# Part of a streamed weight chunk made resident, paid for with one output-tail buffer and a gathered tail

## The chip, the cores and the metric

The kernel runs on one core of one Trainium2 chip. The metric is the device time of one execution in microseconds (us). Every kernel is timed several times. PE is the matmul engine and PEld its weight loads, DVE, ACT and POOL are the vector, scalar and general engines, SP and the DMA queues move data.

## The reference, cut to what matters

The program has two independent parts. Part A, a long convolution by FFT, takes the first 490 us and is not touched. Part B is a recurrence over 64 segments of 32 new tokens, each with 8 memory tokens in front. Each segment needs the memory that the segment before it has produced:

```python
mem = mem0
for s in range(n_seg):                              # 64 segments, strictly one after the other
    h = jnp.concatenate([mem, x[:, 32*s:32*s+32]], axis=1)
    q, k, v = (jnp.einsum('btd,dhe->bhte', h, W) for W in (Wq, Wk, Wv))   # 1024 -> 32 heads x 128
    p = _softmax(where(mask, q @ k^T * scale, -1e9))
    o = jnp.einsum('bhte,hed->btd', p @ v, Wo)      # 32 heads x 128 -> 1024
    mem = o[:, :M, :]                               # rows of the memory tokens
    outs.append(o[:, M:, :])
```

(The two lines with `for W in` and `k^T` are shortened; the meaning is the reference's.) The kernel is compared with the reference by relative error.

## The kernel before

All weights of part B are 64 chunks of 128x2048 bf16, 512 KB each. 43 are resident in SBUF, and the other 21 are listed in `STREAM`; two of these are parked after their first load (`KEPT`), so each segment streams 19 chunks through a ring of six slots. A slot is refilled as soon as PE has used its chunk:

```python
STREAM = (0, 1, 3, 7, 11, 15, 21, 23, 25, 29, 33, 36, 40, 43, 46, 49, 51, 53, 59, 60, 62)
TURN = (6, 4)
INLINE = {1: 0, 3: 1, 5: 0, 11: 1, 12: 0, 14: 1}     # streamed output chunk -> parity of the segment
RING = 6

def fetch():                                        # next streamed chunk into the next free slot
    if loads:
        s, ch = loads.pop(0)
        live[s, ch] = k, t = slot()
        (...).dma_start(t[:], stream_src(ch))

def done(ch):                                       # PE has used ch: its slot is free, fetch again
    if ch in streamed:
        free.append(live.pop((now[0], ch))[0])
        ...
        fetch()
```

The last 8 new tokens of every segment don't depend on the memory, so their projections are made in advance. A segment in the loop handles the other 32 rows (24 new tokens and the memory). It runs the projections K, Q, K, Q, V, V, eight chunks each (two halves `g` of each, on four column tiles of PE), the attention, and an output projection over 16 chunks into `yacc`. The end of a segment is called the **turn** here: `Y` is cast from `yacc`, transposed, written into the next segment's input, and only then can the next first K projection begin.

The output rows of those last 8 tokens take a separate path, the **tail**. Its input is kept in `OTB`, and it is worked off for two segments together (a block of an even and an odd segment), so that one matmul covers 16 rows. There are 32 **heads** of it; one head is four small matmuls and four weight loads:

```python
def head(self, h, w):                               # class Tail
    for dq in range(4):
        nc.tensor.matmul(self.acc[32*dq:32*dq+W, ...], lhsT=self.OTB[:, c, 4*g+i, :], rhs=r,
                         ..., tile_position=(0, 32*dq))
```

20 heads use resident chunks and can run at any time. 12 use streamed ones and must run **inline**, in an output projection while the chunk is there. Before the change a block's tail is spread over the block that follows: at the odd turn 6 resident heads before the transposes of `Y` and 4 after them, 6 inline heads in the next even segment, 6 + 4 resident heads at the even turn, 6 inline heads in the next odd segment. That needs two `OTB` buffers.

```python
# out_proj, after the eight matmuls of a chunk
if tail is not None and 2*hp in tail.left and (ch in streamed or last):
    if last or INLINE[hp] == j:                     # j is 0 in even, 1 in odd segments
        tail.head(2*hp, w); tail.head(2*hp+1, w)
...
nc.scalar.copy(Y[:], yacc[:, 0:256])                # the turn
if j == NB - 1 and not last:
    tail = Tail(OTB, b)                             # its constructor clears the accumulator (DVE)
if tail is not None and not last:
    tail.run(TURN[0])                               # 6 resident heads
if not last:
    fill_mem(pend[s + 1][0], Y)                     # transposes of Y on PE, copy into the next input
...
if tail is not None and not last:
    tail.run(TURN[1])                               # 4 resident heads
```

The scores accumulator and the tail's accumulator share one PSUM tile, `SB`. It is seeded with the mask on DVE (`seed_scores`), before the change at the end of each softmax.

## Time and profile before

| | before |
|---|---|
| time, median of 4 runs | 2195.29 us (2187.41 to 2197.44) |
| span of the profiled run, granted clock | 2190.4 us, 0.971 |
| one segment of the loop | 26.8 us |
| bytes moved by DMA | 804.66 MB |

The first fence is from the page of before: the span, the busy time of PE (with its share and its instruction count), and the DMA rows of the 40 time slices, where a digit is the busy share in tenths.

```profile
span 2190.4 us, 81498 instructions
...
PE 1734.6 (79%) x35636; PEld 927.5 (42%) x35636; DVE 872.0 (40%) x2686; ACT 648.4 (30%) x1139; POOL 436.8 (20%) x1131
...
DMA  9998879889999999999999999999999999999996
GB/s 324 340 341 295 267 274 391 277 293 383 388 379 392 393 356 385 392 391 395 392 387 385 393 391 391 394 395 374 396 393 374 388 383 384 389 394 392 394 389 263
DMA packets 262702, 804.66 MB, mean 367 GB/s; under 512 B 52332, under 2 KB 52364, under 8 KB 262343
```

The reader sees DMA at nine tenths all through the loop and PE busy for 79% of the span. The windows view of the loop (1000 to 2000 us) gives the rate more finely; after the busy times come the granted clock, the DMA share and GB/s:

```profile
1000.00:2000.00 1000.00, 809.80 (x19875) 462.04 (x19867) 362.25 (x1303) 256.27 (x485) 178.99 (x567) 0.99 1.01 389
```

The waits view of before, from 600 to 2100 us (28 blocks), lists what ended an engine's idle time, with the total, the number of times and the longest one. L884 is a projection's matmul, L970 the output projection's, L830 a tail head's, L809 the seeding, L821 the clearing of the tail's accumulator. "issue" means that the profile shows nothing that the engine waited for.

```profile
engine line waited for: us in total, times, longest us
...
PEld L884 <- issue: 214.6, 385, 2.2
...
PEld L970 <- issue: 132.9, 176, 1.9
PE acc L884 <- DMA wring<-WS: 102.6, 233, 1.9
...
PE yacc L970 <- DMA wring<-WS: 47.5, 91, 1.1
...
PE SB L830 <- DVE SB L809: 27.8, 28, 1.2
...
PE yacc L970 <- issue: 23.6, 26, 1.6
...
PE SB L830 <- DVE SB L821: 18.3, 26, 0.7
```

PE waits for streamed chunks.

The last fence is the timeline of before around one odd turn. Columns are the start, the duration, the engine, line and operation, and in brackets the idle time before it with its releaser.

```profile
1696.11 0.37 ACT L1026 CAST Y<-yacc 128x256 bf16<-128x256 f32 x1 [4.26 <-PE yacc L970]
...
1696.77 0.40 PE L830 MATMUL SB<-Wmore,OTB 128*16 128x256 bf16 x8 [0.71 <-DVE SB L821]
...
1697.54 0.29 PE L791 MATMUL tps<-ident,Y 128*128 128x128 bf16 x2
...
1697.75 0.61 PE L830 MATMUL SB<-Wlate,OTB 128*16 128x256 bf16 x16
...
1698.19 0.60 PE L884 MATMUL acc<-wring,rec 128*32 128x512 bf16 x8
```

Four heads follow the transposes of `Y` with no wait, and fill the time in which DVE copies the transposes into the next input. The next projection starts 0.65 us after the transposes. Ahead of the transposes six heads wait for the clearing of the tail's accumulator (0.71 us).

### The profile page before, as it was taken

Reading aid. Unit: us, or ns where it says so; the run is one execution under the profiler, and the core shown is the slowest. Engines: PE = TensorE matmul, PEld = TensorE weight load, DVE = VectorE, ACT = ScalarE, POOL = GpSimd, SP = SyncE. Lnnn points to the kernel's source line nnn. Section 1 sums busy time; section 2 is a strip of 40 time slices with the busy share of each in tenths; the row PEclk is TensorE's granted clock in tenths of the full one; section 3 lists DMA queues with packets and bytes.
Section 4 is the critical chain, followed back from the end, with each engine's and each line's share of the span. In section 5 each row is a group of like instructions: output and inputs, shape, how many; then the busy total and the mean of one; then the engine's idle time right before and its main releaser. Section 6 shows DMA issues by size and latency. Waiting matters only on the chain. (4 is left out here: it accounts for less than half of the span.)

```text
span 2190.4 us, 81498 instructions
## 1 busy us (share of the span) xinstructions
PE 1734.6 (79%) x35636; PEld 927.5 (42%) x35636; DVE 872.0 (40%) x2686; ACT 648.4 (30%) x1139; POOL 436.8 (20%) x1131
## 2 busy tenths in 40 slices
PE   4688888678878878888887887888878888888886
PEld 2232233234444444444444444444444444444444
DVE  9927752023333333333333333333333333333332
ACT  8935521122222222222222222222222222222221
POOL 4013422311111111111111111111111211111111
PEclk9899999889999999999999999999999999999999
DMA  9998879889999999999999999999999999999996
GB/s 324 340 341 295 267 274 391 277 293 383 388 379 392 393 356 385 392 391 395 392 387 385 393 391 391 394 395 374 396 393 374 388 383 384 389 394 392 394 389 263
DMA packets 262702, 804.66 MB, mean 367 GB/s; under 512 B 52332, under 2 KB 52364, under 8 KB 262343
## 3 DMA queue, kind: packets, MB, share of 16 engines
q1 hardware_dynamic: 230008, 725.84, 86.9%
q0 software_dynamic: 27120, 63.11, 8.4%
q10 hardware_dynamic: 5216, 10.49, 1.3%
q8 instruction: 279, 4.57, 0.8%
q14 instruction: 79, 0.65, 0.1%
HBM read 739.92 MB, written 62.39 MB: 366 GB/s over the span
## 5 line engine op out<-in xcount | busy, mean ns | idle before, releaser
L884 PEld LDWEIGHTS <-rec 128*32 128x32 bf16 x12351 | 324.2, 96 | 477.8 <-issue 259.1
L884 PE MATMUL acc<-wring,rec 128*32 128x512 bf16 (+1 forms) x3777 | 375.9, 386 | 141.6 <-DMA wring<-WS 126.4
L893 ACT CAST qkv_sb<-acc 128x512 bf16<-128x512 f32 x384 | 224.8, 585 | 660.8 <-PE acc L884 660.8
L970 PEld LDWEIGHTS <-OT 128*32 128x32 bf16 x8192 | 216.3, 96 | 178.2 <-issue 151.3
L970 PE MATMUL yacc<-wring,OT 128*32 128x256 bf16 x3072 | 153.9, 275 | 98.0 <-DMA wring<-WS 56.4
L884 PE MATMUL acc<-Wmid,rec 128*32 128x512 bf16 x3072 | 225.8, 383 | 0.0
L884 PE MATMUL acc<-Wres,rec 128*32 128x512 bf16 x2816 | 221.2, 380 | 0.0
L830 PEld LDWEIGHTS <-OTB 128*16 128x16 bf16 x4096 | 105.1, 90 | 105.5 <-issue 95.1
L956 ACT CAST OT<-OTp 128x512 bf16<-128x512 f32 x128 | 74.9, 585 | 242.9 <-PE OTp L948 242.9
L986 DVE COPY KT<-tps 128x512 bf16<-128x512 bf16 x64 | 27.2, 424 | 298.6 <-PE tps L899 298.6
L785 POOL DMA_DIRECT2D rec<-REC x64 | 37.5, 585 | 526.6 <-issue 277.2
L957 DVE CAST OTB<-OTp 128x128 bf16<-128x128 f32 x128 | 37.3, 291 | 262.1 <-ACT OT L956 262.1
L736 DVE TENSOR_SCALAR wring<-OTp 128x384 int32<-128x384 int32 x126 | 112.2, 890 | 58.4 <-PE acc L884 52.4
L884 PE MATMUL acc<-pw,rec 128*32 128x512 bf16 x1536 | 130.4, 382 | 0.0
L860 POOL COPY KT<-rec 128x128 bf16<-128x128 bf16 x128 | 38.6, 302 | 427.8 <-PE SB L908 421.9
L845 POOL DMA_DIRECT2D out_dram<-YB x128 | 73.0, 577 | 234.2 <-DVE YB L843 224.0
L914 DVE TENSOR_REDUCE mx<-SB 128x5 f32<-128x200 f32 x128 | 47.1, 368 | 181.4 <-PE SB L908 181.4
L830 PE MATMUL SB<-wring,OTB 128*16 128x256 bf16 x1488 | 78.2, 273 | 39.1 <-DVE SB L809 31.0
L899 PE MATMUL tps<-ident,qkv_sb 128*128 128x128 bf16 x1024 | 101.0, 221 | 8.0 <-ACT qkv_sb L893 0.2
L899 PEld LDWEIGHTS <-qkv_sb 128*128 128x128 bf16 x1024 | 62.6, 97 | 105.0 <-ACT qkv_sb L893 67.5
L970 PE MATMUL yacc<-Wlate,OT 128*32 128x256 bf16 x2048 | 93.4, 273 | 2.9 <-issue 2.7
L1026 ACT CAST Y<-yacc 128x256 bf16<-128x256 f32 x64 | 23.8, 372 | 242.8 <-PE yacc L970 238.9
(229 smaller groups left out, 2690.1 us busy)
## 6 DMA issues: line engine op xcount, KB each, us to landing
wring<-WS SPq DMA_DIRECT2D x1216, 512.0 KB, 7.4
rec<-REC POOLq DMA_DIRECT2D x64, 192.0 KB, 6.1
SK<-s_sb SPq DMA_DIRECT2D x16, 512.0 KB, 4.9
SU<-s_sb SPq DMA_DIRECT2D x16, 512.0 KB, 5.0
Kg<-SK SPq DMA_DIRECT2D x32, 256.0 KB, 4.5
Ug<-SU SPq DMA_DIRECT2D x32, 256.0 KB, 5.6
REC<-stage POOLq DMA_DIRECT2D x16, 512.0 KB, 9.7
zt<-SZ SPq DMA_DIRECT2D x16, 512.0 KB, 8.7
```

The source lines that it names most:

```text
L736: nc.vector.tensor_scalar(out=dst, in0=src, scalar1=0, scalar2=None, op0=ALU.bitwise_or)
L785: nc.gpsimd.dma_start(rec[:], REC[:, s, :])
L830: nc.tensor.matmul(self.acc[32 * dq:32 * dq + W, x - o:y - o], lhsT=self.OTB[:, c, 4 * g + i, :], rhs=r, start=first and not self.seeded, ...
L845: nc.gpsimd.dma_start(bass.AP(outb.tensor, outb.offset + (SEG * NB * self.b + NX) * 2048 + 256 * dq, [[2048 * SEG, NB], [2048, 8], [1, 256 ...
L860: nc.gpsimd.tensor_copy(KT[:, :, :, 32:40], KBs[:, 128 * g:128 * g + 128].rearrange("p (c i t) -> p i c t", c=4, i=4))
L884: nc.tensor.matmul(self.acc[32 * c:32 * c + 32, x - 512 * c:y - 512 * c], lhsT=hT[:, kc, :], rhs=r, start=(kc == 0 and x == 512 * c), stop ...
L893: nc.scalar.copy(sb[:], self.acc[:])
L899: nc.tensor.transpose(tp[:, i * 128:(i + 1) * 128], sb[:, i * 128:(i + 1) * 128], ident[:])
L914: nc.vector.tensor_reduce(out=mx[:], in_=S, op=ALU.max, axis=AX.X)
L956: nc.scalar.copy(OT[:], o_view[:, :, :, 0:32])
L957: nc.vector.tensor_copy(OTB[:, :, 4 * g:4 * g + 4, 8 * j:8 * j + 8], o_view[:, :, :, 32:40])
L970: nc.tensor.matmul(yacc[32 * dq:32 * dq + 32, x - o:y - o], lhsT=OT[:, c, i, :], rhs=r, start=(h == 0 and x == o), stop=(h == 31), tile_po ...
```

## The change

The intent is to stream fewer bytes. The change makes room in SBUF for 768 of the 2048 columns of one streamed chunk (the third, K projection, `order[3]`). It does so by keeping one `OTB` in place of two, by letting the padded softmax tile share the buffers of QT and KT, and by a pool with one buffer. With one `OTB` a tail must be done before the next even segment writes it. So all 12 inline heads run in the odd segment's own output projection, 4 + 6 resident heads at the odd turn, and the last ten between chunk pairs of the next first K projection. `seed_scores` for the next segment moves from the second softmax to behind `fill_mem`, so that the inline heads don't wait for it.

The core of the diff (the buffer sharing of the softmax tile, the store buffer of its own and the end of the last block are cut):

```diff
-TURN = (6, 4)
-INLINE = {1: 0, 3: 1, 5: 0, 11: 1, 12: 0, 14: 1}
+TURN = (4, 6)
+HALF, HELD = 3, 768
...
+    half = order[HALF]
+    WH = ring.tile([128, HELD], BF, name="WH")
+    nc.gpsimd.dma_start(WH[:], dram_chunk(half)[:, 0:HELD])
...
-            (...).dma_start(t[:], stream_src(ch))
+            c = slice(HELD if ch == half else 0, 2048)
+            eng.dma_start(t[:, c], stream_src(ch)[:, c])
...
+        if ch == half:
+            return [(0, HELD, WH[:]), (HELD, 2048, t[:, HELD:2048])]
...
-                    if tail is not None and 2 * hp in tail.left and (ch in streamed or last):
-                        if last or INLINE[hp] == j:
-                            tail.head(2 * hp, w)
-                            tail.head(2 * hp + 1, w)
+                    if j == NB - 1 and ch in streamed:
+                        tail.head(2 * hp, w)
+                        tail.head(2 * hp + 1, w)
...
-            k0 = Proj(0, 0).run().evac()
+            k0 = Proj(0, 0)
+            for n in (3, 3, 32, 0):
+                k0.run(2)
+                more_tail(n)                        # tail.run(n) in even segments
+            k0 = k0.evac()
...
-                OTB_new = one.tile([128, 4, 8, 8 * NB], BF, tag=f"OTB{b % 2}", name="OTB")
+                OTB = one.tile([128, 4, 8, 8 * NB], BF, tag="OTB", name="OTB")
...
+            if j == NB - 1:
                 tail.run(TURN[0])
             if not last:
                 fill_mem(pend[s + 1][0], Y)
+                seed_scores()
...
+            if j == NB - 1:
+                tail.run(32 if last else TURN[1])
```

More of the change, by code (lines that the diff above doesn't have):

```diff
@@ L653, in fetch @@
             live[s, ch] = k, t = slot()
-            (nc.gpsimd if k > 3 and s == 0 and len(live) < 3 else nc.sync).dma_start(t[:], stream_src(ch))
+            c = slice(HELD if ch == half else 0, 2048)
+            eng = nc.gpsimd if k > 3 and s == 0 and len(live) < 3 else nc.sync
+            eng.dma_start(t[:, c], stream_src(ch)[:, c])
     def place(ch, ap):
@@ L712, in b_kernel @@
     one = ctx.enter_context(tc.tile_pool(name="b_one", bufs=1, side="right", reuse_waits="tile"))
-    two = ctx.enter_context(tc.tile_pool(name="b_two", bufs=2, side="right", reuse_waits="tile"))
+    two = ctx.enter_context(tc.tile_pool(name="b_two", bufs=1, side="right", reuse_waits="tile"))
     ps_acc = ctx.enter_context(tc.tile_pool(name="b_ps_acc", bufs=2, space=PSUM))
@@ L774, in done @@
                 fetch()
-    P_pad = one.tile([128, 5, 64], BF, name="P_pad")
-    nc.vector.memset(P_pad[:], 0.0)
     QBm = one.tile([128, 4, 4, 32], BF, name="QBm")
@@ L814, in b_kernel, with __init__ @@
         class Tail:
-            def __init__(self, OTB, b, acc=None):
-                self.OTB, self.b, self.acc = OTB, b, tacc if acc is None else acc
-                self.seeded = acc is None
+            def __init__(self, OTB, b):
+                self.OTB, self.b, self.acc = OTB, b, tacc
                 self.left = list(range(32))
@@ L824, in head @@
                 g, c, i = h // 16, (h % 16) // 4, h % 4
-                first = len(self.left) == 32
                 self.left.remove(h)
@@ L831, in head @@
                                          lhsT=self.OTB[:, c, 4 * g + i, :], rhs=r,
-                                         start=first and not self.seeded, stop=not self.left,
+                                         start=False, stop=not self.left,
                                          skip_group_check=True, tile_position=(0, 32 * dq))
@@ L841, in store @@
             def store(self):
-                YB = one.tile([128, 256], BF, tag="QT", name="YB")
+                YB = one.tile([128, 256], BF, tag="YB", name="YB")
                 nc.vector.tensor_copy(YB[:], self.acc)
@@ L847, in store @@
                                 [[2048 * SEG, NB], [2048, 8], [1, 256]]), YB[32 * dq:32 * dq + W, :])
-        OTB = tail = own = None
+        OTB = tail = None
         for s in range(n_seg):
@@ L910, in scores, with softmax_a @@
                                          tile_position=(0, 32 * c))
-            def softmax_a():
+            def softmax_a(g):
+                P_pad = one.tile([128, 5, 64], BF, tag="KT" if g else "QT", name="P_pad")
+                nc.gpsimd.memset(P_pad[:, 0:4, 32:64], 0.0)
                 mx = two.tile([128, 5], F32, tag="mx", name="mx")
@@ L917, in softmax_a, with softmax_b @@
                 nc.scalar.activation(S, S, ACT.Exp, scale=scale)
-            def softmax_b():
-                ssum = two.tile([128, 5], F32, tag="ssum", name="ssum")
+                return P_pad
+            def softmax_b(P_pad):
+                ssum = two.tile([128, 5], F32, tag="mx", name="ssum")
                 nc.vector.tensor_reduce(out=ssum[:], in_=S, op=ALU.add, axis=AX.X)
@@ L936, in softmax_b @@
                     nc.vector.transpose(out=PT[:, kb, :, 32:40], in_=P_pad[:, 4, ks])
-                seed_scores()
                 return PT
@@ L972, in out_proj, with more_tail @@
                                                  tile_position=(0, 32 * dq))
-                    if tail is not None and 2 * hp in tail.left and (ch in streamed or last):
-                        if last or INLINE[hp] == j:
-                            tail.head(2 * hp, w)
-                            tail.head(2 * hp + 1, w)
-                    if own is not None and ch in streamed:
-                        own.head(2 * hp, w)
-                        own.head(2 * hp + 1, w)
-                    done(ch)
-            k0 = Proj(0, 0).run().evac()
+                    if j == NB - 1 and ch in streamed:
+                        tail.head(2 * hp, w)
+                        tail.head(2 * hp + 1, w)
+                    done(ch)
+            def more_tail(n):
+                if tail is not None and j == 0:
+                    tail.run(n)
+            k0 = Proj(0, 0)
[3 more added lines that the diff above has]
+            k0 = k0.evac()
             q0 = Proj(1, 0).run(4)
@@ L992, in b_kernel @@
             scores(0, QT0, KT0)
-            softmax_a()
+            P0 = softmax_a(0)
+            if j == NB - 1:
+                tail = Tail(OTB, b)
             q1 = Proj(1, 1).run(4)
@@ L997, in b_kernel @@
             nc.scalar.copy(KT1[:, :, :, 0:32], transposes(k1))
-            PT0 = softmax_b()
+            PT0 = softmax_b(P0)
+            seed_scores()
             q1 = q1.run(4).evac()
@@ L1004, in b_kernel @@
             scores(1, QT1, KT1)
-            softmax_a()
+            P1 = softmax_a(1)
             pv1 = Proj(2, 1).run(4)
             if j == 0:
-                OTB_new = one.tile([128, 4, 8, 8 * NB], BF, tag=f"OTB{b % 2}", name="OTB")
-                OTB = OTB_new
+                OTB = one.tile([128, 4, 8, 8 * NB], BF, tag="OTB", name="OTB")
             attend(0, PT0, V0)
             OT0 = evac_o(0)
-            PT1 = softmax_b()
+            PT1 = softmax_b(P1)
             pv1.run(4)
@@ L1017, in b_kernel @@
             yacc = ps_acc.tile([128, 512], F32, tag="acc", name="yacc")
-            if last:
-                own = Tail(OTB, b, ps_acc.tile([128, 512], F32, tag="acc", name="own_acc")[:, 0:256])
             out_proj(range(0, 5), OT0)
@@ L1026, in b_kernel @@
             nc.scalar.copy(Y[:], yacc[:, 0:256])
-            if j == NB - 1 and not last:
-                tail = Tail(OTB, b)
-            if tail is not None and not last:
+            if j == NB - 1:
                 tail.run(TURN[0])
@@ L1032, in b_kernel @@
                 fill_mem(pend[s + 1][0], Y)
+                seed_scores()
             nc.gpsimd.dma_start(bass.AP(outb.tensor, outb.offset + SEG * s * 2048, [[256, 4], [2048, 32], [1, 256]]), Y[:])
-            if tail is not None and not last:
-                tail.run(TURN[1])
-            if last:
-                own.run(32)
+            if j == NB - 1:
+                tail.run(32 if last else TURN[1])
 @with_exitstack
```

## The prediction

> **What bounds the kernel now.** From about 480 us on, the kernel is a loop of 64 segments (the casts of Y end from 490 to 2177 us: 26.8 us each), bound by the 16 DMA engines. The page's slices show DMA at 9 tenths and mostly 375 to 395 GB/s there; in the DMA packet records 16.2 packets are under way on average, and fewer than 8 in only 0.2% of the loop. A segment streams 19 chunks of 512 KB (1216 issues of wring<-WS), 2432 packets of 4096 bytes; at a mean of 168 ns (median 162) over 16 engines this is 25.5 of the 26.8 us; small transfers and instruction fetches fill the rest. PE is busy 79% of the span and waits for wring<-WS (126 us in the projections, 56 us in the output projection). [...]
>
> **What the change removes.** Columns 0 to 767 of the third streamed chunk stay in SBUF: in each segment 128 packets shrink from 4096 to 2560 bytes, 12.6 MB in all. Packets carry a fixed part: the software queue's 3072-byte packets take 131 ns, its 4608-byte ones 186 (medians), so about 21 ns plus 36 ns per 1000 bytes. [...] Estimate for 2560 bytes: 108 to 114 ns. Saved: about 54 ns x 8 packets per engine = 0.42 us a segment, 27 us in 64.
>
> **What it adds and moves.** One matmul a segment (the split column group), two POOL memsets a segment, one 192 KB load: under 1 us. The tail's work keeps its sum but gathers: 12 streamed heads inside the odd segment's output projection, 4+6 at that turn, 10 in the next first K projection; the even turn has none. A head costs PE about 0.11 us. Removed on PE: the wait of the first inline tail head for the score seeding (DVE SB L809, 27.8 us in 28 blocks), the wait for the tail's memset (0.65 us a block), about 1.2 us at each even turn. Added at the odd turn: 6 heads now wait for the seeding (estimate 0.8 us), and 1.1 us of heads among the first K chunks. Sharing QT's and KT's buffers should cost nothing.
>
> **On the critical path: only DMA time.** PE's savings should buy nothing. PE's lateness costs only where the queue runs dry: stream work in flight averages 3 to 4 chunks, but dips to 1.9 (0.4 in the worst tenth) some 2 us after an odd turn, where the change puts the tail's rest. I allow 2 us for that in the whole run.
>
> **Prediction.** 2197 - 27 + 2 = 2172 us, 1.1% faster. Range 2160 to 2184. Faster by over 2%: 0.03; within 2%: 0.96; slower by over 2%: 0.01.
>
> **What would show it.** Bytes moved fall from 804.7 to about 792.3 MB; DMA stays at 9 tenths; 2560-byte packets at 105 to 116 ns; mean period 26.4 us; the wait for SB L809 inside the output projection gone, one at the odd turn new.
>
> **What would make it wrong.** Packets of 2560 bytes costing nearly as much as long ones (gain under 15 us); the queue running dry at odd turns (gain of a few us); a hidden PE limit in the loop, whose relief gains more than the bytes do.

The 0.11 us of a head can be read off before's timeline above, as an estimate: two heads take 0.40 us (L830, x8) and four take 0.61 (x16), so each further one about 0.11.

## The result, and the profile after

| | before | after |
|---|---|---|
| median, runs | 2195.29 us, 4 | 2216.87 us, 4 |
| range | 2187.41 to 2197.44 | 2214.54 to 2223.49 |
| ratio after/before, 95% interval | | 1.0110 (1.0076 to 1.0144) |
| span of the profiled run, clock | 2190.4 us, 0.971 | 2215.6 us, 0.954 |

Ratios here are the mean time of one kernel's fast runs over that of the other's of the same rounds, so they are not quite the ratio of the medians. The change costs 1.1%, about 24 us, where a gain of 1.1% was predicted. It is still within 2%, but far outside the predicted range of 2160 to 2184.

The page of after shows that the bytes did go, exactly as many as predicted (792.30 MB):

```profile
span 2215.6 us, 82009 instructions
...
PE 1771.3 (80%) x35700; PEld 958.4 (43%) x35700; DVE 874.1 (39%) x2683; ACT 649.2 (29%) x1139; POOL 462.6 (21%) x1260
...
DMA  9998889889999999999999999999999999999997
GB/s 326 344 338 285 264 290 392 251 304 359 380 367 356 383 371 373 374 377 375 367 370 371 378 386 374 374 379 389 366 382 391 365 384 369 355 389 377 358 383 289
DMA packets 262769, 792.30 MB, mean 358 GB/s; under 512 B 52348, under 2 KB 52380, under 8 KB 262407
```

The DMA digits are unchanged, while GB/s is lower in nearly every slice of the loop. The windows view of after, 1000 to 2000 us, says the same in one line:

```profile
1000.00:2000.00 1000.00, 817.32 (x19671) 473.74 (x19662) 358.15 (x1283) 252.49 (x477) 190.29 (x627) 0.97 0.99 376
```

376 GB/s in place of 389: DMA is a little less used after the change, although its digit and its share look the same. The packet records show where the engines stood empty: in the three us before an odd turn 14.0 packets are under way on average, against 16.2 in before, and fewer than eight in 10% of that time, against none; in the six us after it 14.5, against 15.6. The queue runs dry around the odd turns, ahead of them as much as behind. So the engines' capacity didn't set the pace there. The short packets themselves were cheap: the packet records give a median of 102 ns for 2560 bytes and of 160 ns for 4096 bytes, better than the 108 to 114 ns that the prediction had.

The waits view of after, 600 to 2100 us (L887, L975, L833 and L814 are the lines that were L884, L970, L830 and L809):

```profile
engine line waited for: us in total, times, longest us
...
PEld L975 <- issue: 170.2, 235, 2.8
...
PEld L887 <- issue: 164.1, 316, 2.1
...
PE acc L887 <- DMA wring<-WS: 70.5, 169, 1.8
...
PE yacc L975 <- DMA wring<-WS: 69.4, 139, 1.9
...
PE yacc L975 <- issue: 38.2, 35, 2.5
...
PE SB L833 <- DVE SB L814: 20.3, 27, 0.8
```

The waits for the seeding inside the output projection and for the clearing are gone, as predicted, and the one at the odd turn is new: 20.3 us / 27 = 0.75 us each (0.8 was estimated). Waits for chunks in the projections fell by 32 us and those in the output projection rose by 22. The unexplained waits of the weight loads rose from 132.9 to 170.2 us in the output projection and fell from 214.6 to 164.1 in the projections. PE's own in the output projection rose from 23.6 to 38.2.

The timeline of after around one odd turn:

```profile
1444.38 0.29 PE L975 MATMUL yacc<-wring,OT 128*32 128x256 bf16 x3 [0.40 <-DVE wring L742]
...
1445.92 0.39 PE L975 MATMUL yacc<-wring,OT 128*32 128x256 bf16 x5 [1.26 <-issue]
...
1447.88 0.37 ACT L1035 CAST Y<-yacc 128x256 bf16<-128x256 f32 x1 [5.02 <-PE yacc L975]
1448.31 0.28 PE L796 MATMUL tps<-ident,Y 128*128 128x128 bf16 x2
...
1448.63 0.19 DVE L797 COPY rec<-tps 128x64 bf16<-128x64 bf16 x1 [4.31 <-PE tps L796]
...
1449.09 0.20 DVE L814 CAST SB<-mask 128x40 f32<-128x40 bf16 x1
...
1449.35 0.83 PE L833 MATMUL SB<-Wlate,OTB 128*16 128x256 bf16 x24 [0.75 <-DVE SB L814]
...
1450.00 0.61 PE L887 MATMUL acc<-wring,rec 128*32 128x512 bf16 x8
```

Two things are to be seen. After the transposes DVE copies them into the next input (ready at 1448.82), then seeds, and the six heads wait for the seeding; the projection, which stands behind them on PE, starts 1.69 us after the transposes, where it took 0.65 us before. But this wait only took the place of another: before's transposes were themselves held up by heads that waited for the clearing. From the start of `Y`'s cast to the projection it is 2.12 us here and 2.08 in before. By the records of 29 odd turns, the projection starts 2.15 us after the end of the cast, against 1.97 in before; at the even turns, which the change emptied, it is 0.64 against 1.32. And near the end of the output projection PE stops between the third and fourth matmul of one chunk for 1.26 us, and the profile shows nothing that it waited for ("issue").

From the first cast of `Y` to the last, the loop takes 1713.0 us in place of 1687.3. By the ends of these casts an even segment takes 27.20 us in place of 26.93, and an odd one 27.18 in place of 26.64. The loss is made in the loop, two thirds of it in odd segments.

### The profile page after: what moved, and what is told of

Read it like the earlier page. It is cut to its first block, busy times and chain, and to the rows that moved or that the text cites. A ratio compares the mean times of both kernels' runs of the same rounds, so it can differ in the third digit from the quotient of the medians.

```text
span 2215.6 us, 82009 instructions
## 1 busy us (share of the span) xinstructions
PE 1771.3 (80%) x35700; PEld 958.4 (43%) x35700; DVE 874.1 (39%) x2683; ACT 649.2 (29%) x1139; POOL 462.6 (21%) x1260
## 2 busy tenths in 40 slices
DMA packets 262769, 792.30 MB, mean 358 GB/s; under 512 B 52348, under 2 KB 52380, under 8 KB 262407
## 4 chain that ended last, share of the span: by engine, by line
DMA 53%; PE 32%; issue 6%; DVE 5%; ACT 2%; SPq 1%; POOL 1%; ACTq 0%; POOLq 0%; DVEq 0%
DMA wring<-WS 44%; PE acc L887 12%; PE SB L833 4%; PE yacc L975 4%; DVE wring L742 4%; PE kb_ps L580 3%; PE vb_ps L700 2%; PE tps L902 2%; DMA SU<-s_sb 2%; DMA VBD<-pair 1%; ACT s_sb L210 1%; DMA Kg<-SK 1%; DMA Kx<-in_A_k_dram 1%; DMA pair<-in_B_x_dram 1%; DMA zt<-SZ 1%
## 5 line engine op out<-in xcount | busy, mean ns | idle before, releaser
L887 PEld LDWEIGHTS <-rec 128*32 128x32 bf16 x12415 | 333.0, 97 | 413.6 <-issue 200.3
L887 PE MATMUL acc<-wring,rec 128*32 128x512 bf16 (+1 forms) x3713 | 388.8, 393 | 106.6 <-DMA wring<-WS 88.2
L975 PEld LDWEIGHTS <-OT 128*32 128x32 bf16 x8192 | 229.4, 98 | 223.9 <-issue 198.7
L975 PE MATMUL yacc<-wring,OT 128*32 128x256 bf16 x3072 | 160.7, 282 | 124.7 <-DMA wring<-WS 84.1
L887 PE MATMUL acc<-Wmid,rec 128*32 128x512 bf16 x3072 | 230.6, 389 | 1.1 <-issue 1.0
L887 PE MATMUL acc<-Wres,rec 128*32 128x512 bf16 x2816 | 221.9, 381 | 0.7 <-issue 0.7
L833 PEld LDWEIGHTS <-OTB 128*16 128x16 bf16 x4096 | 122.5, 93 | 79.3 <-issue 58.6
L1041 POOL DMA_DIRECT2D out_dram<-Y x64 | 46.2, 722 | 502.6 <-ACT Y L1035 479.0
L917 POOL MEMSET P_pad<- 128x128 bf16 x128 | 26.3, 205 | 535.6 <-PE SB L911 528.2
L887 PE MATMUL acc<-pw,rec 128*32 128x512 bf16 x1536 | 129.9, 382 | 0.0
L995 DVE COPY KT<-tps 128x512 bf16<-128x512 bf16 x64 | 27.2, 425 | 202.0 <-PE tps L902 202.0
L797 DVE COPY rec<-tps 128x64 bf16<-128x64 bf16 x64 | 12.3, 192 | 230.4 <-PE tps L796 227.5
L975 PE MATMUL yacc<-Wlate,OT 128*32 128x256 bf16 x2048 | 97.7, 280 | 5.4 <-issue 5.4
```

What stands on the lines that cost most here:

```text
L833: nc.tensor.matmul(self.acc[32 * dq:32 * dq + W, x - o:y - o], lhsT=self.OTB[:, c, 4 * g + i, :], rhs=r, start=False, stop=not self.left, ...
L887: nc.tensor.matmul(self.acc[32 * c:32 * c + 32, x - 512 * c:y - 512 * c], lhsT=hT[:, kc, :], rhs=r, start=(kc == 0 and x == 512 * c), stop ...
L975: nc.tensor.matmul(yacc[32 * dq:32 * dq + 32, x - o:y - o], lhsT=OT[:, c, i, :], rhs=r, start=(h == 0 and x == o), stop=(h == 31), tile_po ...
L1041: nc.gpsimd.dma_start(bass.AP(outb.tensor, outb.offset + SEG * s * 2048, [[256, 4], [2048, 32], [1, 256]]), Y[:])
```

## The experiments

Fifteen kernels ran, each timed in five rounds beside before on the same chip. The tables at the ends of the groups and the numbers called "of the packet records" or "of the PE records" were computed from the traces' records. Sizes in us are the ratio's difference times 2195 us, unless medians are named. Five kernels (e1, e5, e9, e14, e15) leave out or falsify work to measure its cost.

### What are the bytes worth, and where?

**e1** is before with only the bytes taken away. The missing columns are read from another tile, so K is wrong (the comparison passed all the same).

```diff
-            (...).dma_start(t[:], stream_src(ch))
+            c = slice(768 if ch == order[3] else 0, 2048)
+            (...).dma_start(t[:, c], stream_src(ch)[:, c])
...
+        if ch == order[3]:
+            return [(0, 768, WB[:]), (768, 2048, t[:, 768:2048])]
```

> The kernel before with only the bytes taken away: the third streamed chunk is fetched as 1280 of its 2048 columns, and the missing 768 columns are read from another resident tile (wrong result on purpose). Tail, buffers and order as before. Theory A (the stream limits the loop, and the new tail order is what costs): 22 to 30 us faster than before. Theory C (the loop is not limited by bytes, so the saving is worth nothing): within 5 us of before.

Measured: 2195.53 us against 2191.75, ratio 1.0012 (0.9978 to 1.0046). The saving that was put at 27 us is worth nothing, or at most 5 us at the edge of the interval.

**e2** is the converse, after with the chunk streamed whole.

```diff
-            c = slice(HELD if ch == half else 0, 2048)
+            c = slice(0, 2048)
...
-        if ch == half:
-            return [(0, HELD, WH[:]), (HELD, 2048, t[:, HELD:2048])]
```

> The changed kernel with the third chunk streamed whole again, so everything of the change but the bytes. Theory A: the tail order alone costs about 45 to 50 us, so 2235 to 2245 us. Theory C: the bytes are worth nothing, so as the changed kernel, about 2217 us.

Measured: 2221.85 against 2191.75, ratio 1.0124 (1.0094 to 1.0155). Against after's 1.0110 the bytes buy about 3 us, and the intervals overlap. From both sides, the bytes of this chunk hardly count.

**e5** takes the same number of bytes from a chunk that is fetched elsewhere in the segment, `order[43]` of the V projection. Everything else is e1. V is wrong (relative error 0.214).

```diff
-            c = slice(768 if ch == order[3] else 0, 2048)
+            c = slice(768 if ch == order[43] else 0, 2048)
```

> The kernel before with only bytes taken away, as in the first run, but from the streamed chunk of the second V projection instead of the third chunk of the first K projection (wrong result on purpose). Its transfer runs 10 to 17 us after a turn, where the stream moves 400 GB/s; the third chunk's runs at the turn, at 300 to 370. Theory D (bytes are worth time only where the queue is full; at the turn the stream waits for free slots): 12 to 27 us faster than before. Rival (the byte saving is eaten by half-clock spells of the PE, 15 in the loop of the first run against 9 before, wherever the bytes are): within 5 us of before, and again more spells.

Measured: 2178.69 against 2190.63, ratio 0.9946 (0.9922 to 0.9970). Here the same bytes are worth 12 us. The intervals of e1 and e5 don't overlap: the place decides.

Why the place? The packet records give the rate of the stream by the time since the last turn, averaged over the turns of the loop:

```
mean GB/s     -3 to 0 us   0 to 6 us   6 to 9 us   9 to 24 us after the turn
before              392         354         380          402
e1                  361         331         381          402
e5                  380         344         374          398
after               351         334         379          393
```

The stream is slower in the six us after a turn than later, 354 against 402 GB/s in before. PE uses no streamed chunk while it waits for `Y`, so no slot comes free, and the ring has six. The short packets of the K chunk move mainly from 3 us before a turn to 1 us after it (four fifths of them before the turn, where before's rate is still 391); those of the V chunk move 11 to 16 us after it. In e1 the rate falls around the turn by 31 GB/s for 3 us and 23 GB/s for 6 us, which is about 231 KB a segment; 197 KB were saved (128 x 768 x 2 bytes). The whole saving appears as a lower rate around the turn, and no later rate rises. The engines stand idle instead: in e1 the mean number of packets under way falls from 16.2 to 15.3 in the three us before a turn, and from 15.7 to 15.2 in the six us after it. Where the V chunk is fetched, it is 16.3 in before and in e5. That the stream waits for slots there is argued from these rates; that the bytes there are worth nothing is measured.

### What do the moved heads cost?

**e6** is before with one line changed: all 12 inline heads in the odd segment. The bytes, the buffers and the heads at both turns stay.

```diff
-INLINE = {1: 0, 3: 1, 5: 0, 11: 1, 12: 0, 14: 1}
+INLINE = {1: 1, 3: 1, 5: 1, 11: 1, 12: 1, 14: 1}
```

> The kernel before with one constant changed: all six streamed pairs of tail heads run in the odd segment, as in the changed kernel, none in the even one; turns, buffers and bytes as before. If the gathering inside the output projection is a main part of the loss: odd segments about 0.6 us longer and even ones not shorter, 10 to 20 us slower than before. If not: within 5 us of before.

Measured: 2203.98 against 2190.63, ratio 1.0060 (1.0044 to 1.0077), so gathering alone costs 13 us. Even segments get shorter (26.93 to 26.27 us), odd ones longer by more (26.64 to 27.72). In the three us before an odd turn 14.8 packets are under way, against 16.2 in before. The work is the same; moving it from one segment to the next isn't free.

**e3** is after with the seeding put behind the six heads of the odd turn, so that they need not wait for it.

```diff
                 fill_mem(pend[s + 1][0], Y)
-                seed_scores()
...
             if j == NB - 1:
                 tail.run(32 if last else TURN[1])
+            if not last:
+                seed_scores()
```

> The changed kernel with the score seeding placed after the six tail heads at the odd turn instead of before them, so that the heads no longer wait for it. If the wait at the turn is a main part of the loss: first K chunk at the odd turn about 0.8 us earlier, up to 25 us faster (2192). If the gathering of heads in the first K projection is what costs: under 10 us faster.

Measured: 2200.23 against 2191.75, ratio 1.0043 (1.0013 to 1.0074). In the trace the six heads no longer wait (later heads, in the first K projection, still wait for 0.24 us each, 6.6 us in all), and the projection starts 1.38 us after the end of `Y`'s cast, where it took 2.15. In after the wait is worth 1.0110 - 1.0043, about 15 us (give or take 10, by the two intervals), and it sums to 20.3 us over 28 blocks. So in this schedule much of PE's lateness at the turn reaches the end; the prediction had allowed 2 us. But the 15 us are not a share of the loss against before: before's odd turn, with its wait for the clearing, is nearly as long as after's.

**e4** asks for the ten heads in the next first K projection, and moves them to the second one.

```diff
-            k0 = Proj(0, 0)
-            for n in (3, 3, 32, 0):
-                k0.run(2)
-                more_tail(n)
-            k0 = k0.evac()
+            k0 = Proj(0, 0).run().evac()
...
-            k1 = Proj(0, 1).run(4)
+            k1 = Proj(0, 1)
+            for n in (3, 3):
+                k1.run(2)
+                more_tail(n)
```

> The changed kernel with the last ten tail heads moved from the first K projection of the even segment to its second (the K projection of the other half, 8 to 11 us after the turn), where more stream work is in flight. Theory A (heads right behind the turn make PE late and let the DMA queue run dry): first K projection ends 1.2 us earlier, 15 to 30 us faster (about 2190 to 2200). A rival (the heads cost the same wherever they stand, or the loss is in the odd segment's output projection): within 6 us of 2217. A second rival ([...]24 spells in the loop against 8): the time follows the number of half-clock spells.

Measured: 2216.63 against 2191.75, ratio 1.0119 (1.0084 to 1.0155), the same as after. It makes no difference whether the ten heads lie straight behind the turn or one projection later; what they cost in either place isn't measured.

Added up: gathering 13, the wait 15, bytes 0 to -3, together +25 to +28 us, and +24 were measured. That the sum fits is in part luck: the wait took the place of the one for the clearing, and the even turn, 0.68 us shorter, isn't in the sum. Later runs show that such terms don't always add.

**e11** checks whether late seeding alone would help before: `seed_scores` out of the second softmax, to behind `tail.run(TURN[1])`.

```diff
-                seed_scores()                       # end of softmax_b
...
             PT0 = softmax_b()
+            seed_scores()
...
                 tail.run(TURN[1])
+            if not last:
+                seed_scores()
```

> The kernel before with only the seeding of the scores moved from the second softmax to behind the turn's tail heads. It takes away the 1 us that the first tail head in the output projection waits for the seeding. If this wait delays the release of slots: 8 to 20 us faster than before. If it only fills time in which PE would wait for the stream: within 5 us.

Measured: 2188.93 against 2194.77, ratio 0.9988 (0.9957 to 1.0019). The wait of 27.8 us inside the output projection, which the change removes, had been worth nothing measurable. Of two waits of 1.0 and 0.75 us a block, the longer one cost nothing and the shorter one 15 us.

### A rival: the granted clock

The clock of after is lower (0.954 against 0.971). Its records show spells of 3.4 us, some of 6.8, at half clock (a granted share of 0.5): 24 in the loop against 8. In these two traces PE was busy, in the 3.41 us ahead of each spell, for 0.27 to 0.56 of the time (0.81 is the mean of the loop), and in after 15 of the spells lie nearer to an even turn, which the change emptied, than to an odd one (4 of 8 in before). Segments that no spell touches take 26.87 us on average in after (40 of 63) and 26.59 in before (52), the others 27.75 and 27.71. So the spells mark slow segments, but an estimated 0.28 x 63, about 17 of the loop's 26 us, are lost without them (give or take 10, by the scatter of the segments). The clock theory of the expectations is the guess that a lighter load of PE brings the spells and that they cost time. If the spells make the others slow, refilling the even segments should help.

**e7** adds 14 useless heads to after's even segments, before and after the even turn's transposes and in two streamed output chunks; their result is discarded.

```diff
+                    if j == 0 and hp in (5, 12):
+                        dummy((2 * hp, 2 * hp + 1), w)
...
+            if j == 0:
+                dummy(spare[:6])
             if not last:
                 fill_mem(pend[s + 1][0], Y)
+                if j == 0:
+                    dummy(spare[6:10])
```

> The changed kernel with useless PE work added in the even segments alone: 14 heads of matmuls where the kernel before had useful ones (4 in the output projection, 6 and 4 at the turn), into the tail's accumulator before it is cleared, so the result stays right. Clock theory [...]: spells fall from 24 towards 10 to 15 and the kernel gets 5 to 20 us faster though it does 1.5 us more PE work a block. Lateness theory (PE work of a segment is what costs): same or up to 15 us slower.

Measured: 2232.30 against 2190.63, ratio 1.0179 (1.0158 to 1.0200). It is slower than after by 15 us, and 20 spells remain. The clock theory missed, though not yet cleanly, as the spells stayed.

**e9** goes the other way: before without any tail heads in even segments (wrong, relative error 0.318).

```diff
-                        if last or INLINE[hp] == j:
+                        if not last and INLINE[hp] == j == 0:
+                            tail.left.remove(2 * hp)
+                            tail.left.remove(2 * hp + 1)
+                        elif last or INLINE[hp] == j:
...
+            if tail is not None and not last and j == 0:
+                tail.left = [h for h in tail.left if (3, h // 2, 0) not in res]
```

> The kernel before without the tail heads of its even segments (6 in the output projection, 10 at the even turn): strictly less PE work, nothing else changed (wrong result on purpose). Clock theory [...]: half-clock spells in the loop rise from 9 to 18 or more, and the kernel gets no faster, or slower by up to 15 us. Lateness theory (only late PE work costs; the spells are a by-product): same to 15 us faster, with the even turn shorter by 0.7 us.

Measured: 2181.71 against 2194.77, ratio 0.9960 (0.9933 to 0.9987). The spells rise from 8 to 30, and it gets 9 us faster. So more spells need not mean a longer time. But e9 also does less work, so what a spell itself costs isn't measured: within e9's trace the segments that one touches take 27.25 us, and the others 26.23.

**e10** fills PE's waits in a kernel with late seeding (e8, below) with useless matmuls: 28 groups of four a block, where the trace showed PE waiting (the calls are cut).

```diff
+        FILL_HP, FILL_KC = {1: 4, 3: 5, 5: 3, 11: 2, 14: 2}, {1: 3, 3: 4, 7: 3}
+        def fill_pe(y, n):
+            w = res[3, 0, 0]
+            for _ in range(n):
+                for dq in range(4):
+                    nc.tensor.matmul(y[32*dq:32*dq+32, 256:512], lhsT=ident[:, 0:32], rhs=w[:, 0:256],
+                                     ..., tile_position=(0, 32*dq))
```

> The eighth run's kernel (late seeding, resident columns of the V chunk, 34 spells, 126 us at half clock) with useless matmuls only where PE waits anyway in and after the even segment: ahead of streamed chunks of its output projection (16 groups of 0.11 us), 2 groups behind the even turn's transposes, 10 ahead of streamed chunks of the next first K projection; they write to unused columns, so the result stays right. Clock theory: spells fall to about 15, time from 2202 to 2180 to 2192. Lateness theory: 2202 or up to 15 us more.

Measured: 2282.18 against 2194.77, ratio 1.0417 (1.0389 to 1.0446). Both theories missed by far: 78 us more than e8. At 0.11 us a group (the estimate for a head, which has as many matmuls of 256 columns) the filling is an estimated 28 x 32 x 0.11 = 99 us of PE time; although it was put where PE waits, 78 us of it came back as time. This called for a new theory.

### A new theory: the supply of PE instructions

The page lists packets of the kind "instruction" on DMA queue 8, 279 in before (79 more on queue 14); the expectations call them instruction fetches. Those of the loop are 16 KB each, and their number follows the PE instructions (nearly all of them matmuls and weight loads). In 58 segments of the loop there are 61712 over 241 packets in before, 59740 over 233 in e14, 68324 over 267 in e10, 256 to each every time. PE stalls cluster behind these packets. Of before's 225 idle times of PE in the loop that are longer than 0.5 us, 73 end 0.95 to 1.65 us after such a packet has landed; by chance it would be about 11%, 25 of them. In after it is 76 of 161. The stretches of the same width just before and just behind hold only 15 and 27 in before, 10 and 20 in after. The stall of 1.26 us in the timeline above is one: a packet lasted from 1443.37 to 1444.39 us, and PE went on at 1445.92. The theory, called the instruction-supply theory in the expectations: in a packed stretch of small PE instructions it is their number that costs, not PE's busy time. That PE waits for its instructions there is the guess; no run shows it. What the number costs can be tested.

**e13** is e10 with the same idle time filled by one whole-array matmul per group: 2 PE instructions in place of 8.

```diff
-                for dq in range(4):
-                    nc.tensor.matmul(y[32*dq:32*dq+32, 256:512], lhsT=ident[:, 0:32], rhs=w[:, 0:256],
-                                     ..., tile_position=(0, 32*dq))
+                nc.tensor.matmul(y[:, 256:512], lhsT=ident[:], rhs=w[:, 0:256], ...)
```

> The tenth run's kernel (2282 us; useless matmuls in PE's waits cost 80 us) with each group of four 32-column-tile matmuls of 256 columns replaced by one matmul on the whole array of 256 columns: the same PE time a group (about 0.11 us), 2 instructions instead of 8. Instruction-supply theory ([...]what costs is the number of instructions in a dense stretch): cost falls from 80 to under 35 us, so 2205 to 2235. Lateness theory (PE time costs, however it is made up): 2270 to 2290 again.

Measured: 2221.50 against 2191.63, ratio 1.0149 (1.0123 to 1.0176). The pages of e10 and of e13, PE's busy time and instruction count:

```profile
PE 1850.0 (81%) x39253; PEld 1044.6 (46%) x39284; DVE 875.7 (38%) x2683; ACT 648.3 (28%) x1139; POOL 461.5 (20%) x1260
```

```profile
PE 1856.9 (84%) x36596; PEld 984.1 (44%) x36596; DVE 876.2 (39%) x2683; ACT 648.5 (29%) x1139; POOL 461.3 (21%) x1260
```

PE is as busy as in e10, but the filling costs 19 us in place of 78. The 28 x 6 x 32 = 5376 instructions that are gone were worth 59 us, 11 ns each.

**e14** does it to the change itself. It is after, with each of the 12 inline heads done by one whole-array matmul (wrong; it only keeps the shape of the work): 24 PE instructions a block in place of 96.

```diff
-                for dq in range(4):
-                    ... nc.tensor.matmul(self.acc[32*dq:32*dq+W, ...], lhsT=self.OTB[:, c, 4*g+i, :], ...)
+                nc.tensor.matmul(self.acc, lhsT=ident[:], rhs=w[0][2][:, 0:256], ...)   # inline heads only
```

> The changed kernel with each of the 12 gathered tail heads in the odd segment's output projection done as one whole-array matmul of 256 columns instead of four column-tile ones: same PE time, 24 instructions for a segment's twelve heads instead of 96 (wrong result on purpose). Instruction-supply theory: the stalls that end 1.0 to 1.6 us after an instruction fetch in the odd segment's last stretch (1.13 us a segment, 0.44 before) fall back to about 0.5, odd segments get 0.4 to 0.8 us shorter, 2195 to 2206. Lateness theory: within 6 us of 2217.

Measured: 2182.42 against 2191.63, ratio 0.9972 (0.9935 to 1.0010). From the page of e14:

```profile
PE 1773.8 (81%) x34548; PEld 912.1 (42%) x34548; DVE 872.2 (40%) x2683; ACT 648.1 (30%) x1139; POOL 461.7 (21%) x1260
```

PE is busy for 1773.8 us, against 1771.3 in after, yet the time falls by 1.0110 - 0.9972, 30 us: more than the whole loss. 2304 instructions are gone, at 13 ns each. The waits view of e14, 600 to 2100 us, shows PE's own unexplained idle time in the output projection (38.2 us in after):

```profile
PE yacc L978 <- issue: 11.2, 16, 1.7
```

e14 also no longer reads `OTB` in those heads, but in after's waits view these heads wait for no `OTB`, so that is not where the gain comes from.

**e15** is e14 with e3's late seeding (wrong in the same way).

```diff
 e14, and:
-                seed_scores()                       # behind fill_mem
...
+            if not last:
+                seed_scores()                       # behind tail.run(TURN[1])
```

> The same on top of the third run's late seeding (2200 us). If the wait for the seeding and the dense stretch in the odd segment are the whole loss: back to before or a little below it, 2180 to 2195. Lateness theory: 2200 again.

Measured: 2188.25 against 2191.63, ratio 0.9997 (0.9969 to 1.0025). Late seeding, worth 15 us in after, is worth nothing here. The terms don't add: with the gathered heads as few instructions it gains nothing that the projection starts 1.07 us after the end of `Y`'s cast at the odd turn and not 1.87 (e14).

Here is the sum of the PE stalls of more than 0.3 us that end 0.95 to 1.65 us after an instruction packet, over 58 segments; beside it the part in the last stretch of odd segments, from 24 us after the turn, and the half-clock spells of the loop.

```
            stalls, us: even + odd    end of odd segments, us each    spells
before             34 + 43 =  77                  0.44                     8
after              42 + 52 =  94                  1.13                    24
e3                 45 + 47 =  92                  1.06                    17
e6                 30 + 47 =  77                  0.76                     8
e10               111 + 61 = 172                  1.14                    30
e13                60 + 55 = 115                  1.00                    15
e14                30 + 15 =  45                  0.04                    11
e15                38 + 15 =  53                  0.05                    18
```

At the end of after's odd segments, where the inline heads stand closest, these stalls grow from 0.44 to 1.13 us, and in e14 they disappear. But the table doesn't settle all: e6 loses 13 us with an unchanged sum. And spells fall along with the instructions. In segments that no spell touches e14 is 0.26 us shorter than after (26.87 to 26.61), about half of the 33 us by which its loop is shorter; e13 is 0.54 shorter than e10 (27.45 to 26.91), more than half of 57. So the 11 and 13 ns include what the spells cost.

### Is there a version that beats both?

**e8** puts the two lessons on top of after: late seeding (e3), and the resident columns from the V chunk.

```diff
 e3, and:
-HALF, HELD = 3, 768
+HALF, HELD = 43, 768
```

> The changed kernel with the late seeding of the third run and the resident three eighths taken from the streamed chunk of the second V projection. Theory D: 12 to 25 us faster than the third run (2200), so 2175 to 2188 and below before. Rival (bytes are worth nothing anywhere): 2200 again.

Measured: 2202.56 against 2190.63, ratio 1.0061 (1.0038 to 1.0083), no better than e3. In this schedule the V chunk's bytes buy nothing either. It has 33 spells, the most of all. The segments that none touches take 26.04 us, against 26.56 in e3, so the bytes may be worth something that the spells take away again. No run tested this; it stays open.

**e12** keeps before's spread tail and its two `OTB` buffers, and takes only the room that costs nothing: the shared softmax tile and the pool with one buffer. That holds 512 columns of the V chunk. It also has e11's late seeding.

```diff
 e11, and after's sharing of the softmax tile with QT and KT, and:
+HALF, HELD = 43, 512
...
+            c = slice(HELD if ch == half else 0, 2048)
...
+        if ch == half:
+            return [(0, HELD, WH[:]), (HELD, 2048, t[:, HELD:2048])]
```

> A version meant to beat both: the kernel before with its spread tail and two output-tail buffers, late seeding, the padded probabilities in the QT and KT buffers as in the changed kernel, and in the space that this frees 512 columns of the second V projection's streamed chunk resident. Bytes give two thirds of the 12 us of the fifth run (8 us), the seeding what the run beside it shows: 8 to 25 us faster than before, 2168 to 2184.

Measured: 2179.08 against 2194.77, ratio 0.9944 (0.9918 to 0.9970), correct, 796.42 MB. It beats before by 12 us and after by 1.6% (0.9944 over 1.0110), with fewer bytes saved than the change saves.

## Why the prediction was wrong

It was wrong: 2172 us were predicted, 2216.87 measured. Point by point:

1. *"Saved: about 54 ns x 8 packets per engine = 0.42 us a segment, 27 us in 64."* This step failed. The first half was right, even cautious: the packets take 102 ns against 160 ns. (An estimate from these two sizes puts the fixed part at about 5 ns a packet; the 21 ns came from another queue.) The second half took a saving of engine time for a saving of time. It rests on *"bound by the 16 DMA engines"*, and that was read from shares over the whole loop. It doesn't hold around the turn, where the chosen chunk is fetched: without its bytes the engines stand idle there (e1: 15.3 packets under way in place of 16.2), and nothing later comes sooner. Measured: nothing (e1), about 3 us within the noise (e2), and 12 us for the same bytes elsewhere (e5), still not 27.

2. *"16.2 packets are under way on average, and fewer than 8 in only 0.2% of the loop"* was true and misled. The mean duration of a 4096-byte packet is 194 to 200 ns some 4 us after the turn, and 163 ns later: the count stays nearly full there (15.8) because the packets last longer. The bytes that arrive per us tell what the count hides. What holds the stream has to be asked of each stretch of a segment.

3. *"PE's lateness costs only where the queue runs dry ... I allow 2 us"* and *"PE's savings should buy nothing."* This step failed too, in size and in place. The queue does run dry, as the prediction's last paragraph feared, but more than it allowed, and ahead of an odd turn as much as behind it (fewer than eight packets under way in 10% of the three us ahead and 4% of the six us behind); the prediction had looked only behind. Gathering the heads, counted as the same sum of work, costs 13 us by itself (e6), about half of the 24 us of the result. The new wait was foreseen to the tenth (0.75 us, 0.8 estimated), and called free; taking it out of after gains 15 us (e3), though it is about as long as the wait that it replaced. PE's savings bought nothing in e11, but 9 us in e9. How the rest of the 24 us is made up isn't shown.

4. Missing altogether was a cost per PE instruction, though "a hidden PE limit in the loop" was named as a possibility; it was expected to help. Lines of idle time called "issue" were the largest that the fence of before's waits shows. With the same busy time on the page, e14 has 2304 fewer instructions and gains 30 us, e13 has 5376 fewer and gains 59 over e10. These two pairs show that packed small matmuls cost more time than whole-array ones that keep PE as busy. That it is their number, and not their column-tile form, is argued from the similar cost of one (13 and 11 ns). That their supply in 16 KB packets is the reason is the guess, from the count of 256 to a packet and from the stalls behind the packets; no run changed the supply itself, so it isn't shown.

5. Right were: the bytes (792.3 MB), DMA still at nine tenths, the loss of the seeding wait inside the output projection, the new one at the odd turn, and, as far as is seen, that buffer sharing costs nothing (e12 has it and is the fastest correct version). The doubt about heads in the first K projection was not needed: moving them to the second changes nothing (e4). The mean period was predicted as 26.4 us and is 27.2.

Open are five points: why gathering costs 13 us in e6 while the sum of its stalls behind instruction packets doesn't grow (77 us, as in before); why the V chunk's bytes bring 12 us and not 27 in e5, and nothing in e8; how much of the 15 us of the odd turn's wait comes through instructions, since it vanishes when the instructions do (e15); how the loss beyond the 13 us of gathering is made up; and what the half-clock spells cost by themselves.

## What to carry to other kernels

Price a saving of bytes in the stretch in which those bytes move: where the stream waits for something (here presumably for slots), the bytes taken away were worth nothing (e1, ratio 1.0012). Count instructions as well as busy time where an engine runs many small ones (2304 fewer at the same busy time were worth 30 us in e14), and ask what stands behind idle time for which the profile shows no wait. Before work is gathered into one stage because its sum stays the same, try the move alone: here one changed line showed half of the loss.
